# The first block's keys and queries with token groups outermost over the partitions

## The chip, the cores and the metric

The kernel runs on one core of a Trainium2 chip. A core has a matrix engine (PE, or TensorE), a vector engine (DVE), a scalar engine (ACT), GpSimd (POOL) and SyncE (SP), and moves data with 16 DMA engines. The metric is the device time of one execution in microseconds. Times of before and after are medians of several runs.

## The reference

Causal sliding-window attention with a linear distance bias, followed by a two-layer MLP with a squared ReLU. Cut to what matters:

```python
B, H, S, D = q.shape                       # 8, 8, 576, 64
scores = scale * q @ k.T                   # scale = 1 / sqrt(D)
bias = slopes[h] * -abs(i - j)
scores = where((i >= j) & (i - j < 128), scores + bias, -1e9)
attn = softmax(scores)
x = (attn @ v).transpose(0, 2, 1, 3).reshape(B * S, H * D)   # 4608 x 512
h = maximum(x @ w_in, 0.0)                 # w_in: 512 x 2048
out = (h * h) @ w_out                      # w_out: 2048 x 512
```

All inputs and the output are float32; the kernel computes in bfloat16 with float32 accumulation.

## The kernel before

The 576 tokens of each of the 8 batches are cut into four blocks of 128 and one of 64, which gives 40 blocks. Block numbers 0 to 7 are the first blocks of the eight batches (they attend only to themselves), the others follow by pairs of batches. For a block, q, k and v are loaded for all 8 heads with tokens on the partitions (tile `kq`, 128 x 1024, keys in the first half and queries in the second; `vf` or `vt` for the values). Keys and queries are transposed so that the head dimension lies on the partitions (`kqf` or `kqT`), the scores are formed (`s`, L499), exponentiated (L523), multiplied with a table of decays (`masks`), multiplied with the values (`pv`, L566), divided by their row sum into `x` and transposed again into `xT`. The MLP then works on groups of 512 tokens: an up-projection (`h`, L700 in units of 128 or 256 tokens for the first groups, L716 afterwards), ReLU and square into `g`, and a down-projection (`o`, L742).

The order of all instructions is written out when the program is built. Class `Plan` holds every task with its engine, an estimated duration, its dependencies and the ring buffers that it takes, and simulates the engines to choose an order; the tasks are then emitted in this order. The order, and the number of filler matmuls that `fill` puts on PE in planned gaps of the first 30 us (L252, on a zeroed tile `warm`), depend on the planner's estimates alone.

The list `FIRST` sets the order of the first loads: blocks 0 to 3 come ahead of the weights, then the quarters of w_in and w_out mixed with block 4, then blocks 5 to 7. Loads of GpSimd (queue q0) convert from float32 to bfloat16 on the way; at most eight of them are in flight, and a ninth waits for the first (`LANES`).

Block 0 differs. Its keys and queries are fetched as float32 into the tile `stage` by four loads (L373): keys and queries, each in two halves, one half on SP's queue and one on ACT's. VectorE then casts them into `kq` (L379), PE transposes them (L443), and `evac` (L451 to L458) copies the transposes into `kqf`. In `source` the 128 tokens are split into 32 groups g of four tokens i, and the eight heads into four pairs c of two heads r. A partition of `stage` holds one pair c and one group g: four tokens of 64 numbers, which is one run of 1 KB in memory for each head of the pair. Which partition it is follows from the order of c and g:

```python
        if split:
            return s.rearrange("(c r) (g i) d -> c g r (i d)", r=2, i=4)
```

So partition 32 c + g holds head pair c and token group g. After the transposes, the columns of the PSUM tile are in this order too, once for each i, and the evacuation sorts them into token order. The destination of a load is the 128 partitions of `stage`, 256 numbers in each.

Of the kernel before, what the change touches and what calls it, by code (L numbers as in the profile page):

```python
# [175 lines left out]
def kernel(  # L176
# [14 lines left out]
    C = d_model // 128  # L191
# [54 lines left out]
    def bank_of(slot, name):  # L246
        bank(slot, name)
        return slot

    def fill(task, slot):  # L250
        for _ in range(int(task.gap * FILL / 56.0) if task.gap > 200.0 else 0):
            nc.tensor.matmul(slot.tile[:, 0:128], warm[:, 0:128], warm[:, 0:128], start=True, stop=True)  # L252

    def tile_of(slot):
        return tiles[slot.tag][slot.idx]

    def act(n):
        return n * 0.95 + 115.0
# [4 lines left out]
    def dve_p(n, rate=1):  # L263
        return n / rate / 0.96 + 185.0

    def mm(n):
        return max(n, 66) / 2.4 + 2.5

    def copy(task, o, i):
        if task.eng == "DVE":  # L270
            nc.vector.tensor_copy(o, i)  # L271
        else:
            nc.scalar.activation(o, i, AF.Copy)  # L273
# [76 lines left out]
    def source(t, m, split=False):  # L350
        b, kb = seq[m]
        s = t[b, :, kb * 128:kb * 128 + blk[kb], :]
        if split:
            return s.rearrange("(c r) (g i) d -> c g r (i d)", r=2, i=4)
        return s.rearrange("h s d -> s h d")

    def load_block(m, key):
# [10 lines left out]
        if m == 0:  # L368
            t_l = []
            for i, src in enumerate((k, q)):  # L370
                for r, (eng, e) in enumerate((("SP", nc.sync), ("ACTQ", nc.scalar))):
                    def fetch(i=i, src=src, r=r, e=e):
                        e.dma_start(view(stage, i)[:, r], source(src, m, split)[:, :, r])  # L373
                    t_l.append(plan.add({eng: 450.0}, key + 0.1 * i, fetch, dma=330.0, lat=1000.0,
                                        name=f"l{'kq'[i]}{m}.{r}"))

            def cast_kq(i):
                w = slice(i * d_model, (i + 1) * d_model)
                nc.vector.tensor_copy(kq[s_kq[m].idx][:, w].rearrange("s (i r d) -> s r i d", i=4, d=D),  # L379
                                      stage[:, w].rearrange("s (r i d) -> s r i d", r=2, d=D))  # L380
            c_k = plan.add({"DVE": 480.0}, key, lambda: cast_kq(0), t_l[0:2], [s_kq[m]], name=f"ck{m}")
            c_q = plan.add({"DVE": 480.0}, key, lambda: cast_kq(1), t_l[2:4] + [c_k], name=f"cq{m}")
            t_kq[m] = [c_k, c_q]
        else:
            def fetch_kq():
                for i, src in enumerate((k, q)):
                    nc.gpsimd.dma_start(view(kq[s_kq[m].idx], i), source(src, m, split))  # L387
            t_kq[m] = [plan.add({"POOL": 1780.0}, key, fetch_kq, [], [s_kq[m]], dma=2 * ns,
                                name=f"lkq{m}", count=2)]

        def fetch_v():
            nc.gpsimd.dma_start(tile_of(s_v[m])[0:n, :, 0:D], source(v, m))  # L392
# [29 lines left out]
    def transpose_kq(m, due):  # L422
        n = blk[seq[m][1]]
        kb = seq[m][1]
        sT = s_kqT[m] = Slot("kqT" if kb else "kqT0")
        split = m == 0
        if m >= N_PE:
            def flip():
                nc.sync.dma_start_transpose(out=tile_of(sT)[:, :, 0:n], in_=kq[s_kq[m].idx][0:n, :])
            t_f = plan.add({"SP": 1500.0}, due - 60, flip, t_kq[m] + [t_zero if kb == HALF else None], [sT],  # L430
                           [s_kq[m]], dma=1700.0 * n / 128, name=f"kqT{m}")
            t_kqT[m] = [[t_f], [t_f]]
            return
        t_tp, evs = [None, None], [[], []]
        for i in range(2):
            st = Slot(TP if m else "o")

            def tp(i=i, st=st):
                fill(t_tp[i], bank_of(st, "tp"))
                st.tile = st.tile.bitcast(BF16)  # L440
                src = kq[s_kq[m].idx][:, i * d_model:(i + 1) * d_model]
                for j in range(C):
                    nc.tensor.transpose(st.tile[:, j * 128:(j + 1) * 128],  # L443
                                        src[:, j * 128:(j + 1) * 128], ident)
            t_tp[i] = plan.add({"PE": 4 * mm(128)}, due - 60 + i, tp,
                               [t_ident, t_tp[0] if i else last["tp"], t_kq[m][min(i, len(t_kq[m]) - 1)]],
                               [st] if i else [st, sT], [s_kq[m]] if i else [], name=f"tp{m}.{i}")

            pieces = [(0, C // 2), (C // 2, C)] if i and m == 0 else [(0, C)]
            for c0, c1 in pieces:  # L450
                def evac(i=i, st=st, c0=c0, c1=c1, e=len(evs[i])):  # L451
                    o = tile_of(sT)[:, i * C + c0:i * C + c1, 0:n]
                    if split:
                        src = st.tile[:, 0:512].rearrange("p (i c g) -> p c g i", i=4, c=C)[:, c0:c1]
                        o = o.rearrange("p c (g i) -> p c g i", i=4)
                    else:
                        src = st.tile[:, 0:512].rearrange("p (c s) -> p c s", c=C)[:, c0:c1, 0:n]
                    copy(evs[i][e], o, src)  # L458
                w = (c1 - c0) * n
                evs[i].append(plan.add({"ACT": act(w), "DVE": dve_p(w, 1 if split else 2)}, due - 58, evac,  # L460
                                       [t_tp[i]] + evs[i], [], [st], name=f"ev{m}.{i}"))
        last["tp"] = t_tp[1]
        t_kqT[m] = [[evs[0][0], evs[1][0]], evs[0] + evs[1]]
# [339 lines left out]
```

## Time and profile before

| | before |
|---|---|
| time, median of 3 runs | 321.18 us (320.49 to 322.58) |
| span of the profiled execution | 320.1 us |
| PE busy | 304.7 us (95%) |
| weight loads of PE (PEld) busy | 177.6 us (55%) |
| DVE busy | 175.3 us (55%) |
| ACT busy | 168.8 us (53%) |
| POOL busy | 105.4 us (33%) |
| moved by DMA | 39.54 MB |

A matmul's end is modelled, so the busy time of PE is an upper figure for useful work, and filler matmuls count as busy. In the parts of the profile shown below, a line of the chain of waits has start, length and what it was; a line of the timeline has start, length, engine, line of the kernel, operation, output and input, and in brackets the idle time before it and what ended it. A queue line has the number of packets, the megabytes and the time of its packets as a share of 16 engines' span.

### The profile page before, as it was taken

How to read it: one execution, taken by the hardware profiler on the slowest of the kernel's cores; microseconds unless marked ns; L12 is line 12 of the kernel's file. 1: busy time of each engine (PE TensorE's matmuls, PEld its weight loads, DVE VectorE, ACT ScalarE, POOL GpSimd, SP SyncE). 2: the span in 40 equal slices, each digit the busy share in tenths (PEclk: the TensorE clock that was granted, in tenths of full speed). 3: DMA queues.
4: the chain of work that ended last, by engine and by line, in shares of the span. 5: the costliest groups of instructions: out<-in, count | busy, mean ns of one | idle time of the engine just before them, and what ended most of it. 6: DMA issues, size and time to landing. Idle time of an engine off the chain costs nothing.

```text
span 320.1 us, 7110 instructions
## 1 busy us (share of the span) xinstructions
PE 304.7 (95%) x2776; PEld 177.6 (55%) x2820; DVE 175.3 (55%) x495; ACT 168.8 (53%) x324; POOL 105.4 (33%) x131
## 2 busy tenths in 40 slices
PE   4698999999999999999999999999999999999994
PEld 1596876777767645555545455554554444444442
DVE  2366446867767766677676667675764222222211
ACT  3356466666776327766666666645662444344300
POOL 8652579364352864411955105500000000000000
PEclk9999999999999999999999999999999999999998
DMA  9999999999999999997999929991121100010112
GB/s 105 122 200 202 189 160 188 145 158 166 159 157 166 187 176 163 156 164 141 151 187 170 161 67 156 161 163 52 38 60 37 66 33 33 37 33 33 66 68 66
DMA packets 165682, 39.54 MB, mean 124 GB/s; under 512 B 156304, under 2 KB 161168, under 8 KB 165648
## 3 DMA queue, kind: packets, MB, share of 16 engines
q0 software_dynamic: 114656, 18.10, 87.2%
q1 hardware_dynamic: 50728, 20.72, 34.7%
q8 instruction: 22, 0.36, 0.5%
q10 hardware_dynamic: 264, 0.26, 0.3%
q14 instruction: 12, 0.10, 0.1%
HBM read 36.70 MB, written 9.44 MB: 144 GB/s over the span
## 4 chain that ended last, share of the span: by engine, by line
PE 92%; DMA 3%; ACT 1%; issue 1%; DVE 1%; ACTq 0%
PE o L742 38%; PE h L716 25%; PE h L700 13%; PE pv L566 6%; PE s L499 5%; DMA stage<-in_q_dram 3%; PE tp L443 1%; PE tp L252 1%; ACT P L523 1%; PE xp L608 1%; ACT rt L671 1%; PE pv L252 0%; ACTq L373 0%; PE s L252 0%; PE xp L252 0%
## 5 line engine op out<-in xcount | busy, mean ns | idle before, releaser
L742 PE MATMUL o<-w_out_sb,g 128*128 128x512 bf16 (+2 forms) x568 | 138.8, 373 | 2.7 <-DVE g L662 1.1
L671 ACT ACTIVATE rt<-h 128x512 bf16<-128x512 f32 x144 | 86.2, 608 | 94.8 <-PE h L716 64.1
L662 DVE TENSOR_TENSOR g<-rt 128x512 bf16<-128x512 bf16 x144 | 60.0, 421 | 70.2 <-ACT rt L671 70.0
L716 PE MATMUL h<-xT,w_in_sb 128*128 128x512 bf16 x364 | 95.4, 379 | 0.9
L742 PEld LDWEIGHTS <-g 128*128 128x128 bf16 x592 | 54.2, 98 | 57.7 <-DVE g L662 1.4
L523 ACT ACTIVATE P<-s 128x512 bf16<-128x512 f32 (+1 forms) x132 | 66.5, 595 | 16.0 <-PE s L499 16.0
L716 PEld LDWEIGHTS <-w_in_sb 128*128 128x128 bf16 x384 | 35.0, 98 | 38.8
L531 DVE TENSOR_TENSOR P<-P,masks 128x512 bf16<-128x512 bf16 (+1 forms) x104 | 42.1, 413 | 15.4 <-ACT P L523 11.2
L700 PE MATMUL h<-xT,w_in_sb 128*128 128x128 bf16 (+1 forms) x512 | 46.4, 246 | 0.0
L392 POOL DMA_DIRECT2D vt<-in_v_dram x32 | 27.1, 850 | 54.0 <-PE pv L566 44.9
L387 POOL DMA_DIRECT2D kq<-in_k_dram x39 | 33.6, 860 | 28.8 <-DMA kqT<-kq 21.1
L700 PEld LDWEIGHTS <-w_in_sb 128*128 128x128 bf16 x512 | 38.3, 98 | 4.7 <-issue 0.4
L387 POOL DMA_DIRECT2D kq<-in_q_dram x39 | 33.7, 863 | 9.5 <-DMA w_out_sb<-in_moe_w_out_dram 3.6
L588 DVE TENSOR_TENSOR x<-pv,rec 128x256 bf16<-128x256 f32 (+1 forms) x80 | 33.7, 422 | 2.9 <-DVE rec L584 0.3
L566 PEld LDWEIGHTS <-P 128*128 128x128 bf16 (+1 forms) x576 | 26.0, 101 | 13.9 <-DVE x L588 1.7
L584 DVE RECIPROCAL rec<-pv 128x4 f32<-128x4 f32 (+1 forms) x80 | 14.2, 178 | 19.8 <-PE pv L566 17.6
L566 PE MATMUL pv<-vt,P 128*128 128x65 bf16 (+1 forms) x448 | 24.3, 194 | 0.2
L271 DVE COPY osb<-o 128x512 f32<-128x512 f32 (+2 forms) x17 | 11.2, 661 | 17.0 <-PE o L742 16.8
L273 ACT ACTIVATE osb<-o 128x512 f32<-128x512 f32 x20 | 11.9, 597 | 9.3 <-PE o L742 9.0
L499 PEld LDWEIGHTS <-kqT 64*128 64x128 bf16 x448 | 12.4, 94 | 7.4 <-issue 7.4
L499 PE MATMUL s<-kqT 64*128 64x128 bf16 (+1 forms) x256 | 15.6, 210 | 0.0
L443 PE MATMUL tp<-ident,kq 128*128 128x128 bf16 x64 | 6.2, 242 | 5.8 <-DVE kq L379 5.7
(41 smaller groups left out, 108.1 us busy)
## 6 DMA issues: line engine op xcount, KB each, us to landing
out_dram<-osb SPq DMA_DIRECT2D x32, 256.0 KB, 5.0
kq<-in_k_dram POOLq DMA_DIRECT2D x31, 128.0 KB, 7.5
kq<-in_q_dram POOLq DMA_DIRECT2D x31, 128.0 KB, 7.6
vt<-in_v_dram POOLq DMA_DIRECT2D x24, 128.0 KB, 7.1
w_in_sb<-in_moe_w_in_dram POOLq DMA_DIRECT2D x4, 512.0 KB, 13.4
w_out_sb<-in_moe_w_out_dram POOLq DMA_DIRECT2D x4, 512.0 KB, 14.2
vf<-in_v_dram POOLq DMA_DIRECT2D x8, 128.0 KB, 9.3
out_dram<-osb SPq DMA_DIRECT2D x6, 128.0 KB, 5.3
```

The costliest lines, as they stand in the source:

```text
L387: nc.gpsimd.dma_start(view(kq[s_kq[m].idx], i), source(src, m, split))
L392: nc.gpsimd.dma_start(tile_of(s_v[m])[0:n, :, 0:D], source(v, m))
L499: nc.tensor.matmul(sS[2 * g2 + r].tile[:, jj * 256 + c0:jj * 256 + c0 + w], tile_of(s_kqT[mk])[rows, c, :], tile_of(s_kqT[mq])[rows, C + c ...
L523: nc.scalar.activation(flat(Pt[sP.idx]), sS[i].tile.rearrange("p (j t) -> p j t", j=2)[:, :, lo:hi], AF.Exp, bias=0.0, scale=scale)
L531: nc.vector.tensor_tensor(flat(Pt[sP.idx]), flat(Pt[sP.idx]), flat(masks), op=ALU.mult)
L566: nc.tensor.matmul(sv.tile[0:n, hi * (D + 1):(hi + 1) * (D + 1)], Pt[sP.idx][:, place(h)].rearrange("p t q -> p (t q)")[:, w], tile_of(s_v ...
L588: nc.vector.tensor_tensor(xt[sx.idx][0:n, hf * 256:(hf + 1) * 256].rearrange("p (h e) -> p h e", h=4), heads(sv)[0:n, :, 0:D], sr.tile[0:n ...
L662: nc.vector.tensor_tensor(o, i, i, op=ALU.mult)
L671: nc.scalar.activation(srt.tile, slot.tile, AF.Relu, bias=0.0, scale=1.0)
L700: nc.tensor.matmul(slot.tile[:, f * w:(f + 1) * w], w_in_sb[:, cc, fc * 128:(fc + 1) * 128], xT[:, cc, lo:lo + w], start=cc == 0, stop=cc ...
L716: nc.tensor.matmul(slot.tile, w_in_sb[:, cc, fc * 128:(fc + 1) * 128], xT[:, cc, g * 512:(g + 1) * 512], start=cc == 0, stop=cc == C - 1)
L742: nc.tensor.matmul(slot.tile[:, 0:hi - lo], gt[:, fc, t * 128:(t + 1) * 128], w_out_sb[:, fc, lo:hi], start=fc == 0, stop=fc == FCB - 1)
```

## The change

In the source view of block 0 the order of c and g is exchanged, so that partition 4 g + c holds head pair c and token group g, and the slowest dimension of the loads' source has 32 entries instead of 4. This is meant to let these loads use all 16 DMA engines. The evacuation of the transposes reads its columns in the new order. Nothing else differs: the planner gets the same estimates and so writes the same order, and the load order with four blocks ahead of the weights stands already in the kernel before.

```diff
         if split:
-            return s.rearrange("(c r) (g i) d -> c g r (i d)", r=2, i=4)
+            return s.rearrange("(c r) (g i) d -> g c r (i d)", r=2, i=4)
         return s.rearrange("h s d -> s h d")
...
                     if split:
-                        src = st.tile[:, 0:512].rearrange("p (i c g) -> p c g i", i=4, c=C)[:, c0:c1]
+                        src = st.tile[:, 0:512].rearrange("p (i g c) -> p c g i", i=4, c=C)[:, c0:c1]
                         o = o.rearrange("p c (g i) -> p c g i", i=4)
```

## The prediction
> **What bounds the kernel now.** I read the page's chain first, then the same chain restricted to the first 45 us in order of time. The page:
>
> ```profile
> PE 92%; DMA 3%; ACT 1%; issue 1%; DVE 1%; ACTq 0%
> ```
>
> TensorE bounds the run, and the 3% of DMA is one single piece at the start. The chain in order of time (start us, us, what):
>
> ```profile
> 0.74 1.16 ACTq L373
> 1.90 0.03 issue
> 1.93 8.69 DMA stage<-in_q_dram
> 10.62 0.02 issue
> 10.64 0.44 DVE kq L379
> 11.09 0.05 issue
> 11.13 0.61 PE tp L443 x4
> ...
> 22.34 0.27 PE h L252 x3
> 22.62 1.79 PE h L700 x32
> ```
>
> Block 0's queries take until 10.62 to land; then cast, transpose, and from 11.13 on the chain stays on PE until the first up-projection. Is PE doing work there or waiting? The table by stretches (us, then busy us and instruction count of PE, PEld, DVE, ACT, POOL, the granted clock, DMA share, GB/s):
>
> ```profile
> 4.80:11.13 6.33, 0.61 (x4) 0.35 (x5) 1.41 (x3) 0.77 (x4) 3.76 (x6) 1.00 2.08 182
> 11.13:17.31 6.18, 6.18 (x64) 5.79 (x65) 3.06 (x10) 2.47 (x7) 5.87 (x8) 1.00 1.40 112
> 17.31:22.45 5.14, 5.14 (x99) 4.57 (x97) 3.77 (x17) 3.08 (x8) 2.93 (x4) 1.00 1.26 202
> 22.45:45.00 22.55, 21.26 (x316) 18.34 (x318) 12.94 (x45) 13.34 (x30) 10.41 (x13) 1.00 1.66 187
> 45.00:320.00 275.00, 267.93 (x2295) 147.48 (x2332) 153.09 (x416) 146.93 (x272) 78.44 (x95) 1.00 1.18 117
> ```
>
> PE is busy 0.61 of the 6.33 us before 11.13, and without a gap from 11.13 to 22.45 (76 of those matmuls are the fillers of L252, whose number is fixed when the program is built). Afterwards it is 94% and 97% busy. So a shift of the moment 11.13 is a shift of everything, unless a load that does not shift comes in the way.
>
> **Why the queries are late.** The queues of the first 12 us (packets, MB, share of 16 engines):
>
> ```profile
> q0 software_dynamic: 7066, 0.89, 116.5%
> q10 hardware_dynamic: 264, 0.26, 8.1%
> q1 hardware_dynamic: 264, 0.26, 7.1%
> ```
>
> Each hardware queue carries two of the four 128 KB loads of block 0. 256 packets are the 1 KB rows; the other 8 are 4-byte completion writes, four per load. So each load runs on four engines. In the trace's completion records the last k load lands at 6.87 and the last q load at 10.62. The same records show what this does to the GpSimd loads: of the 16 shares of block 0's v, twelve land from 4.92 to 5.73 and four from 10.47 to 10.80. Those four engines then work off their backlog: about 0.85 us per 128 KB load and 2.55 us per 512 KB load, so the last shares of w_in's first quarter land at 20.79, those of the first w_out quarter at 23.34. A load counts as landed with its last share. The GpSimd line of the timeline shows it too:
>
> ```profile
> 7.58 0.94 POOL L387 DMA_DIRECT2D kq<-in_k_dram  x1
> 11.08 0.88 POOL L387 DMA_DIRECT2D kq<-in_q_dram  x1 [2.57 <-DMA vf<-in_v_dram]
> ```
>
> The ninth load waits 2.57 us for v0, the first of the eight that are in flight.
>
> [...] the clock record starts at 17.31, 6.2 us after PE's unbroken work begins, and fillers go from 0.107 us each to about 0.06. [...] the first cast took 0.92 us while GpSimd issued loads, the second 0.43 while it waited.
>
> **The change, part by part.**
>
> Source view. With g (32) outermost, [...] same 512 rows of 1 KB, same four instructions, issued at the same times. Load time: a 1 KB packet takes 0.046 us on an engine (most of the packet records), so 512 packets are 23.6 us of engine time, 5.9 us on four engines and 1.5 us on sixteen. The first packet goes out at 2.20, and between 2.26 and 3.97 single packets take 0.4 to 1.38 us; I leave a stall of 0.5 to 1.4 us on every engine. The k loads then end near 2.2 + 0.75 + (0.5 to 1.4), plus about 0.3 us from last packet to completion: 3.75 to 4.65, I take 4.35. The q loads need another 0.75 us and meet GpSimd's packets, which begin at 3.59; between 6.3 and 10 the hardware packets went at 61 ns instead of 48 beside those. 4.6 to 6.5; I take 5.2.
>
> Casts on VectorE. Both now fall in a time when GpSimd issues without pause, so I charge 0.92 for each (0.43 is the other bound): k 4.35 to 5.27, q 5.27 to 6.2. Transpose of the queries starts at 6.3 instead of 11.13: **4.8 us earlier**; with 0.43 for the casts and an early q 5.5, with q at 6.5 3.6.
>
> Evacuation of the transposes (L454). Source step of g from 1 to 4 and of c from 32 to 1 elements; the innermost step stays 128, and so do instruction and element count. 0.69 on VectorE and 0.66 for the two on ACT stay; no row shows another stride, [...] I take 0.
>
> GpSimd loads. The four engines lose 5.8 us of block (start at 9.75, counted back from 20.79 by 10 x 0.85 + 2.55), and all sixteen get about 1 us of HW packets that still lie after 3.6. The twelve free engines landed the eighth load by 11.85; two more at 0.86, the weights at 2.55, and 0.5 to 1 us of sharing give 16.6 to 17.1 for w_in's first quarter: **4.2 us earlier** than 20.79 (3.7 to 4.7). The wait of 2.57 us disappears, as v0 lands by about 6.5 while the ninth load comes up at 8.5. Queued behind it are v3 and all weights, which move with it.
>
> Does the PE then meet the weights? In before it uses each well after landing: first quarter in 20.79, used 22.45 (1.65 spare); w_out's second quarter in 28.42, used 29.69 (1.3, the least); w_in's fourth in 38.82, used about 40.4 (1.6). So PE can move 4.2 + 1.3 = 5.5 us; 4.8 fits, with 0.7 left. Block 1's k and q (11.46 and 12.30) come at about 7 to 8.3, their transposes want them at 9.0; block 3's q comes near 13.4 and is wanted at 14.6. Those waits are covered.
>
> [...]
>
> Output stores, DMA transposes and all later loads are untouched and follow PE; the group loop from 45 us on has 97% PE and nothing new to wait for. Sum: 321.18 - 4.8 + 0.1 for small losses = 316.5.
>
> **The rivals.**
> 1. Forecast, 0.68: 316.5.
> 2. More, 0.12: fast casts, q near 4.6[...] move PE by more than the weights allow; the limit is 5.5 to 6: 315.4. For it: the second cast's 0.43. Against: GpSimd no longer pauses.
> 3. Part of it, 0.12: q lands near 7 because GpSimd's packets hold it up on every engine, or the weights move only 1.5 us and PE catches up with them: 1.5 + 1.3 = 2.8, so 318.4. For it: 61 ns against 48. Against: on the four shared engines the hardware packets kept most of the throughput.
> 4. Hidden anyway, 0.04: a wait that I don't see keeps the first up-projection at 22.45: 321.2. Against: PE has no gap from 11.13 on.
> 5. Slower, 0.04: [...] If every newly touched pair costs a stall like the four seen at the start (0.49, 1.38, 0.42 and 0.62, mean 0.73), that is 16 for the four loads: q lands at 2.2 + 1.5 + 16 x 0.73 + 0.3 = 15.7, 5.1 later than now, and the time is 326.3. Against: the other three loads touch new heads too, and after 4.3 no hardware packet takes more than 0.1 us.
>
> **How the numbers follow.** Cases 1 and 2 are faster by over 1% (3.2 us): 0.80. Cases 3 and 4 are within: 0.16. Case 5: 0.04. The range holds 1 with its ends (gains of 3.6 to 5.5), 2, and nearly all of 3: 314.9 to 318.6, which leaves out cases 4 and 5 and tails.
>
> **What would show it.** Right: 288 packets in each hardware queue (256 + 2 x 16), q landing near 5, the tp transposes of block 0 near 6.3, no wait of GpSimd for v0, the first up-projection near 17.6, PE busy as long as before in all. A first L700 near 17.6 with a gap in PE before it would say the weights bind (case 3). Wrong: stage still landing after 8, or PE gaps of more than 1 us between 18 and 45.

## The result and the profile after

| | before | after |
|---|---|---|
| time, median | 320.94 us (320.49 to 322.58, 4 runs) | 318.03 us (317.12 to 318.91, 4 runs) |
| ratio to before, 95% interval | | 0.9900 (0.9853 to 0.9947) |
| the same, measured again later | 321.29 us (11 runs) | 318.29 us (6 runs), ratio 0.9898 (0.9873 to 0.9923) |
| span of the profiled execution | 320.1 us | 316.7 us |

The change makes the kernel 2.9 us faster. The forecast was 4.7 us (316.5 us, range 314.9 to 318.6). The intervals of the two measurements leave 1.7 to 4.7 us and 2.5 to 4.1 us for the gain.

The loads do what they were meant to do. The queues of the first 12 us of the kernel after, columns as before:

```profile
q0 software_dynamic: 9001, 1.14, 148.5%
q1 hardware_dynamic: 288, 0.26, 7.9%
q10 hardware_dynamic: 288, 0.26, 7.9%
```

288 packets are 256 rows and 32 completions, sixteen for each load. And GpSimd's queue has moved 9001 packets instead of 7066 in the same 12 us. The last share of the keys lands at 3.55 us (6.87 before), that of the queries at 6.24 (10.62). All sixteen shares of block 0's v land from 4.71 to 6.71, where four of them had waited until 10.80. GpSimd's line of the timeline no longer has the wait for the ninth load:

```profile
8.43 0.95 POOL L387 DMA_DIRECT2D kq<-in_q_dram  x1
9.30 0.95 POOL L392 DMA_DIRECT2D vf<-in_v_dram  x1
10.16 0.84 POOL L340 DMA_DIRECT2D w_in_sb<-in_moe_w_in_dram  x1
```

The chain of the page shows what became of it:

```profile
PE 80%; DMA 14%; POOL 4%; issue 0%; DVE 0%; POOLq 0%; SPq 0%
```

Before, PE held 92% of the chain and DMA 3%, one load of block 0. Now DMA has 14%. That the number is larger doesn't mean more DMA time; it means that PE now waits for DMA somewhere late enough for the chain to run back through it. Restricted to 40 to 62 us and put in order of time, the chain says where:

```profile
40.47 0.85 POOL kq L387
41.32 7.53 DMA kq<-in_q_dram
...
48.93 9.20 DMA kqT<-kq
58.13 0.04 issue
58.17 0.62 PE s L499 x16
```

The scores of block 8, the first block that is transposed by DMA and not by PE, wait for that transpose. In the kernel before this wait did not exist. PE's own lines in the timeline show it, after two smaller waits for weights that are new as well:

```profile
17.28 1.96 PE L700 MATMUL h<-xT,w_in_sb 128*128 128x128 bf16 x32 [0.82 <-DMA w_in_sb<-in_moe_w_in_dram]
...
24.95 1.02 PE L742 MATMUL o<-w_out_sb,g 128*128 128x512 bf16 x4 [0.26 <-DMA w_out_sb<-in_moe_w_out_dram]
...
58.17 0.23 PE L499 MATMUL s<-kqT,kqf 64*128 64x128 bf16 x2 [1.36 <-DMA kqT<-kq]
```

PE has the same 2820 weight loads in the same order in both kernels, so the start of each can be compared between two traces, and the difference is how far PE is ahead at that moment. After against the first profile of before:

| place | before, us | after, us | ahead by, us |
|---|---|---|---|
| transpose of block 0's queries (L443) | 11.13 | 7.06 | 4.07 |
| transpose of an x tile, the second of them (L608) | 21.50 | 15.34 | 6.16 |
| first up-projection (L700) | 22.40 | 17.28 | 5.12 |
| second quarter of w_out (L742) | 29.69 | 24.95 | 4.74 |
| an up-projection before block 8's scores (L700) | 55.57 | 50.82 | 4.75 |
| block 8's scores (L499) | 61.49 | 58.17 | 3.32 |
| near the end (L742) | 313.79 | 310.33 | 3.46 |

So PE was ahead by some 4.75 us, close to the 4.8 of the forecast, from 25 us to 58 us, and lost 1.4 at one wait. But the table ends at 3.46 and the medians differ by 2.9, so this comparison isn't yet the whole account. The experiments are about both points.

### The profile page after: what moved, and what is told of

It is laid out like the page before. It is cut to its first block, busy times and chain, and to the rows that moved or that the text cites. A ratio compares the mean times of both kernels' runs of the same rounds, so it can differ in the third digit from the quotient of the medians.

```text
span 316.7 us, 7154 instructions
## 1 busy us (share of the span) xinstructions
PE 305.4 (96%) x2820; PEld 175.3 (55%) x2820; DVE 175.2 (55%) x495; ACT 169.0 (53%) x324; POOL 105.4 (33%) x131
## 4 chain that ended last, share of the span: by engine, by line
PE 80%; DMA 14%; POOL 4%; issue 0%; DVE 0%; POOLq 0%; SPq 0%
PE o L742 35%; PE h L716 27%; PE h L700 8%; PE pv L566 5%; DMA w_in_sb<-in_moe_w_in_dram 5%; PE s L499 5%; DMA vf<-in_v_dram 3%; DMA kqT<-kq 3%; DMA kq<-in_q_dram 2%; POOL kq L387 2%; POOL vf L392 1%; POOL w_out_sb L343 1%; POOL w_in_sb L340 0%; POOL dist L287 0%; DVE osb L271 0%
## 5 line engine op out<-in xcount | busy, mean ns | idle before, releaser
L742 PE MATMUL o<-w_out_sb,g 128*128 128x512 bf16 (+2 forms) x592 | 142.9, 374 | 1.3 <-DVE g L662 1.1
L716 PE MATMUL h<-xT,w_in_sb 128*128 128x512 bf16 x384 | 96.9, 380 | 0.0
L742 PEld LDWEIGHTS <-g 128*128 128x128 bf16 x592 | 54.2, 98 | 58.1 <-DVE g L662 1.4
L523 ACT ACTIVATE P<-s 128x512 bf16<-128x512 f32 (+1 forms) x132 | 66.5, 595 | 17.1 <-PE s L499 17.0
L700 PE MATMUL h<-xT,w_in_sb 128*128 128x128 bf16 (+1 forms) x512 | 46.4, 246 | 0.8 <-DMA w_in_sb<-in_moe_w_in_dram 0.8
L700 PEld LDWEIGHTS <-w_in_sb 128*128 128x128 bf16 x512 | 38.3, 98 | 5.5 <-DMA w_in_sb<-in_moe_w_in_dram 1.0
L499 PEld LDWEIGHTS <-kqT 64*128 64x128 bf16 x448 | 12.5, 94 | 7.4 <-issue 7.0
L499 PE MATMUL s<-kqT 64*128 64x128 bf16 (+1 forms) x256 | 15.6, 210 | 0.0
L499 PE MATMUL s<-kqT,kqT 64*128 64x128 bf16 (+1 forms) x192 | 11.4, 210 | 0.0
```

Source lines behind the costliest of these rows:

```text
L499: nc.tensor.matmul(sS[2 * g2 + r].tile[:, jj * 256 + c0:jj * 256 + c0 + w], tile_of(s_kqT[mk])[rows, c, :], tile_of(s_kqT[mq])[rows, C + c ...
L523: nc.scalar.activation(flat(Pt[sP.idx]), sS[i].tile.rearrange("p (j t) -> p j t", j=2)[:, :, lo:hi], AF.Exp, bias=0.0, scale=scale)
L700: nc.tensor.matmul(slot.tile[:, f * w:(f + 1) * w], w_in_sb[:, cc, fc * 128:(fc + 1) * 128], xT[:, cc, lo:lo + w], start=cc == 0, stop=cc ...
L716: nc.tensor.matmul(slot.tile, w_in_sb[:, cc, fc * 128:(fc + 1) * 128], xT[:, cc, g * 512:(g + 1) * 512], start=cc == 0, stop=cc == C - 1)
L742: nc.tensor.matmul(slot.tile[:, 0:hi - lo], gt[:, fc, t * 128:(t + 1) * 128], w_out_sb[:, fc, lo:hi], start=fc == 0, stop=fc == FCB - 1)
```

## The experiments

Theory A was: the gain is given back at block 8's scores. Rival B: the stream of loads came only 3.5 us earlier and holds PE to that, so that another wait for a load or a DMA transpose takes the place of this one within some 10 us. The first four kernels belong together.

**Taking away the wait at block 8.** The scores of block 8 read another block's transposes, which are there already.

```diff
+                                ka, qa = (0 if x == 8 and ms[0] == 8 else x for x in (mk, mq))
                                 nc.tensor.matmul(sS[2 * g2 + r].tile[:, jj * 256 + c0:jj * 256 + c0 + w],
-                                                 tile_of(s_kqT[mk])[rows, c, :], tile_of(s_kqT[mq])[rows, C + c, 0:w],
+                                                 tile_of(s_kqT[ka])[rows, c, :], tile_of(s_kqT[qa])[rows, C + c, 0:w],
```

> The changed kernel, except that the scores of block 8 (its own and those against its predecessor) read the transposes of block 0 in place of block 8's own; block 8's output and what follows from it is therefore other. Same instructions in the same order, but the first score matmuls no longer wait for the DMA transpose of block 8. Theory A (the gain of 4.75 us that PE has at 57 us is given back at that one wait): PE stays about 4.7 us ahead of the kernel before past 58 us, and the time is 316.4 to 316.9, 1.1 to 1.5 less than the changed kernel. Rival B (the whole stream of loads came only 3.5 us earlier and holds PE to that anywhere): another wait for a load or a DMA transpose takes its place within some 10 us, PE is 3.4 to 3.6 ahead afterwards, and the time is 317.7 to 318.3.

Measured: 318.10 us, ratio 0.9899 (0.9870 to 0.9928), as the changed kernel, and in B's range. But in its trace PE is 4.70 us ahead of the first profile of before at 58 us and still at 86, as A says; then it loses 0.53 at an up-projection at 91 us and 0.4 at a score matmul at 116 us. PE's waits from 60 to 125 us in this kernel (total, times, longest, in us):

```profile
PE h L701 <- DMA xT<-x: 0.5, 1, 0.5
PE o L743 <- issue: 0.3, 2, 0.2
```

The new wait is for a DMA transpose again, this time of x. The loss at 116 us is too short for this list; the chain leads from it over VectorE's writing of `x` to a DMA transpose of `x` that landed at 114.56. So A in its narrow form falls: with this wait gone, others of the same kind take its place. B named such waits too, but within 10 us, and these came 33 and 58 us later.

**Bringing the transpose forward.** The values of blocks 5 to 7, which aren't needed before about 46 us, are loaded after block 8's keys and queries. The emission is rearranged once the planner is done, so PE, VectorE and ACT keep their order.

```diff
     done = plan.order()
+    late = [t for t in done if t.name in ("lv5", "lv6", "lv7")]
+    done = [t for t in done if t not in late]
+    z = [t.name for t in done].index("lkq8") + 1
+    done[z:z] = late
```

> The changed kernel with the GpSimd loads of the values of blocks 5, 6 and 7 issued after the keys and queries of block 8 instead of before; everything else in the same order. Block 8's queries should land about 3 x 0.86 = 2.6 us earlier, near 46.2. Theory A1 (the transpose follows the landing of the queries): kqT of block 8 lands near 55.5, before PE wants it at 56.8, the wait of 1.36 us is gone, time 316.4 to 316.9. Theory A2 (the transpose's packets can't start before the backlog of GpSimd's loads has drained, at about 53 us in the changed kernel, and that moment stays): the transpose is issued 2.6 us earlier and still lands at 57 to 58, time 317.5 to 318.3.

Measured: 317.34 us, ratio 0.9880 (0.9853 to 0.9907), which lies between the two ranges, so the trace has to decide. The SP queue of this kernel in the timeline issues the transpose of block 8 at 44.30 instead of 48.93:

```profile
44.30 1.35 SPq L429 DMA_TRANSPOSE kqT<-kq  x1
```

It lands at 52.48, 8.2 us after its issue; in the kernel before that took 8.2 and in the kernel after 9.2. The transpose follows the landing of the queries, which come at 44.21 (A1); a fixed moment at which GpSimd's backlog is drained (A2) is not what it waits for. And PE's waits from 10 to 125 us have no transpose among them, neither block 8's nor a later one:

```profile
PE o L742 <- DVE g L662: 1.1, 1, 1.1
PE h L700 <- DMA w_in_sb<-in_moe_w_in_dram: 0.9, 1, 0.9
PE o L742 <- issue: 0.5, 3, 0.2
```

**The same in the kernel before,** as a control.

> The kernel before with the same later loads of the values of blocks 5 to 7. Theory A: in before the transpose of block 8 landed 1.8 us ahead of its use, so earlier loads are worth nothing: 320.6 to 321.3, no change. Rival B (the stream of loads held PE in before as well): 0.5 to 2 us faster, 319.0 to 320.4.

Measured: 321.23 us, ratio 1.0004 (0.9991 to 1.0016). Without the change, earlier transposes are worth nothing. The wait for block 8's is one that the change brought within reach.

**Half of the change.** Only the keys in the new order.

```diff
-            return s.rearrange("(c r) (g i) d -> g c r (i d)", r=2, i=4)
+            return s.rearrange("(c r) (g i) d -> g c r (i d)" if t is k else "(c r) (g i) d -> c g r (i d)", r=2, i=4)
...
-                        src = st.tile[:, 0:512].rearrange("p (i g c) -> p c g i", i=4, c=C)[:, c0:c1]
+                        src = st.tile[:, 0:512].rearrange("p (i c g) -> p c g i" if i else "p (i g c) -> p c g i", i=4, c=C)[:, c0:c1]
```

> Only the keys of block 0 in the new order, the queries in the old one, so the query loads run on four engines again. If the time on shared engines counts packet by packet: 64 packets on each of four engines at 0.046 to 0.061 us from about 3.1 us on, so the queries land at 6.5 to 7.5, transposed from about 7.9 (11.13 before, 7.06 after), and those four engines start GpSimd's loads near 6.7 (9.75 before): w_in's first quarter lands at 17.8 to 18.5 and the time is 318.0 to 319.2. Rival (what counts is only that no load is confined to four engines; two confined loads cost as much as four): the queries land after 9.5 and the time is 320.3 to 321.2.

Measured: 319.36 us, ratio 0.9942 (0.9919 to 0.9964), just above the range of the first theory, and far from the rival's. Each hardware queue has 276 packets (256 + 16 + 4). The queries land at 8.47, later than the 7.5 allowed for, and w_in's first quarter at 18.73. The dose counts: with two confined loads the ratio lies at 0.9942, with none at 0.9900, so two cost a little under half of what four do. In this trace no load holds PE up: its first up-projection starts at 19.86, 1.1 us after the quarter landed. What binds there is the later queries and PE's own work, with a full clock from 14.29 us on.

These four leave a gap: even without any wait for a transpose the gain is 3.6 us, not 4.7. One suspect is the yardstick, since the first profile of before, at 321.89 us, was 0.9 slower than the median. Two kernels were run again for a second profile.

> The kernel before once more, for a second execution with a profile. Its first profile had the full clock only from 17.31 us, and its time of 321.89 is 0.9 above the median of 320.97. Theory C [...]: with the full clock earlier, the first up-projection starts earlier than 22.45, but not before w_in's first quarter lands at about 20.8, and the span is 319.0 to 319.5. Rival: the clock comes at another time and the span stays within 0.3 of what the start of the up-projection gives otherwise, that is, the 0.9 us lie elsewhere in the run.

Measured: 321.17 us, span 319.4. In this execution PE had the full clock from 14.89 us, not from 17.31. The first up-projection starts 1.28 us earlier than in the first profile, at

```profile
21.17 1.95 PE L700 MATMUL h<-xT,w_in_sb 128*128 128x128 bf16 x32
```

with w_in's first quarter landed at 20.65. And PE's waits from 10 to 125 us have one that the first profile of this same program did not have:

```profile
PE o L742 <- DMA w_out_sb<-in_moe_w_out_dram: 0.5, 1, 0.5
```

Half of the 1.28 us is lost there; 0.58 is left at 29 us and 0.73 at the end. So the span is as theory C says, and the trace says more than expected: the loads can bind PE in the kernel before as well. The kernel before with the later values has the same wait in its trace, 0.6 us long. The 1.3 us that PE seemed to have in hand at the second quarter of w_out belonged to that one execution: just ahead of that place PE is 1.28 us earlier in the second profile, which uses them up, and the quarter landed 0.65 us later (29.07 against 28.42), which makes the wait.

How much of the 0.9 us the clock explains is less sure. The record has the mean granted clock of 54 more executions of the kernel before. In 33 of them it is below 0.99, as in the second profile (0.988); their median is 321.11 us. In the other 21 it is 0.995 or more, as in the first profile (0.996); their median is 321.27. Over many executions the difference is thus about 0.2 us, and in one of the three sessions it goes the other way.

> The changed kernel once more, for a second execution with a profile. Theory: the first up-projection again waits for w_in's first quarter (start 17.2 to 17.6 unless the clock comes after about 11 us), and what is given back is given back at waits for DMA transposes (kqT at 58 us, or xT at about 88 and 112 us), of a size that varies from run to run by up to 1.5 us; span 315.3 to 317.1. Rival: the wait of 1.36 us at block 8's scores is the same in each execution.

Measured: 317.57 us, span 315.8. Its first up-projection waits 0.97 us, for a w_in quarter that landed at 18.19 (17.23 in the first profile of after), so it starts at 18.23 and not at 17.2 to 17.6; block 8's transpose lands at 56.17, before it is wanted, and nothing is lost at 58 us or at any later transpose. So the theory had the span and the varying size right, but not the start, and the rival falls. The trace of the first profile of after shows the difference: fifteen of the sixteen shares of that transpose had landed by 56.74 and one at 58.13. So the size of what is given back varies, and in that execution it hung on a single late share. Against the second profile of before, PE is ahead by (the rows "timed again" are the profiles of two of the last three kernels below):

| | first up-projection | second w_out quarter | block 8's scores and to the end |
|---|---|---|---|
| after, first profile | 3.84 | 4.16 | 2.73 |
| after, second profile | 2.89 | 3.59 | 3.59 |
| after, timed again | 2.95 | 3.63 | 3.64 |
| values later, first profile | 3.64 | 4.38 | 4.38 |
| values later, timed again | 3.42 | 4.15 | 4.15 |

So in two of the three traces of the changed kernel no transpose holds PE up. These three executions took 318.46, 317.57 and 317.52 us; what the slower executions lose beyond that, up to 319.04, has no trace.

**Is it the clock that the change bought?** The kernel before with PE kept busy until the queries land:

```diff
-        for _ in range(N_WARM):
+        for _ in range(30):
```

> The kernel before with 30 warm-up matmuls instead of 8 at the start of PE, emitted without telling the planner, so that PE is busy until 9 to 11 us, where it otherwise waits for the queries, [...]. Theory (weights cap the gain): PE reaches the first up-projection at 20.8 to 21.2, waits there for w_in's first quarter (20.8), and the time is 320.4 to 321.0, at most 0.6 below the kernel before. Rival (the clock, not the loads, is what the change really bought): 318 to 319.5.

Measured: 322.21 us (21 runs), ratio 1.0016 (0.9999 to 1.0032), which is neither's range: no gain, perhaps a loss. The full clock comes at 4.76, and PE's waits from 10 to 125 us show how the earlier start is used up:

```profile
PE o L742 <- DVE g L662: 1.7, 2, 1.1
PE tp L443 <- DVE kq L379: 1.1, 1, 1.1
PE h L700 <- DMA w_in_sb<-in_moe_w_in_dram: 0.5, 1, 0.5
PE o L742 <- issue: 0.5, 3, 0.2
PE s L499 <- DMA kqT<-kq: 0.4, 1, 0.4
PE h L700 <- DMA xT<-x: 0.2, 1, 0.2
```

It is the pattern of the changed kernel, without the earlier loads: PE comes sooner and meets weights and transposes that do not. Ahead of the second profile of before by 1.26 us at the second x transpose, it is 0.48 behind from 95 us on. Why it ends behind was not settled. But an early clock alone brings no gain, so it is not what the change bought.

**Is it the stream of loads that binds at the start?** On top of the later values, one load is left out.

```diff
+    done = [t for t in done if t.name != "lv3"]
...
-                                         tile_of(s_v[mk])[:, h, 0:D + 1], start=mk == parts[0][1], stop=mk == m)
+                                         tile_of(s_v[2 if mk == 3 else mk])[:, h, 0:D + 1],
+                                         start=mk == parts[0][1], stop=mk == m)
```

> The kernel with the values of blocks 5 to 7 loaded later, and block 3's values not loaded at all (its attention reads block 2's values instead, so block 3's output is other). It takes 0.85 us of work out of the stream of loads ahead of the weights and changes nothing else. Theory D (in the first 30 us the stream of loads bounds the changed kernel, PE waits for each weight quarter): all weights land 0.85 us earlier, PE follows, 316.3 to 316.9, against 317.34 with only the later loads. Rival (PE and VectorE's own chain bounds it, the waits for weights are by-products): 317.2 to 317.6.

Measured: 316.93 us, ratio 0.9868 (0.9856 to 0.9881). In time this is in theory D's range, but the step is not clear of noise: the ratio is 0.0012 below that of the kernel with the later values, some 0.4 us, and the two intervals overlap. PE's waits from 10 to 125 us now have no DMA in them at all:

```profile
PE o L743 <- DVE g L663: 1.1, 1, 1.1
PE o L743 <- issue: 0.5, 3, 0.2
```

w_in's first quarter landed at 15.81 and PE used it at 17.03, so PE's own chain took over as the bound there (the full clock came at 11.13 in this execution). That the loads bind the changed kernel at its start is shown by the traces rather than by this time: in all three profiles of it, and in both with the values later, the first up-projection has waited 0.8 to 1.0 us and starts about 0.05 us after that quarter has landed, at 17.28 to 18.23. By these waits PE's own chain stands about a microsecond behind the loads as a bound.

**A version to keep.** The last three were timed side by side.

> The changed kernel, timed beside the next two: 317.6 to 318.4, as in its first measurement.

Measured: 318.29 us, ratio 0.9898 (0.9873 to 0.9923).

> The changed kernel with the values of blocks 5 to 7 loaded after the keys and queries of block 8, timed again beside the changed kernel: 317.1 to 317.6. Theory: 0.5 to 0.9 below the changed kernel, since the wait for block 8's DMA transpose and those after it are gone. Rival: the earlier difference was between two measurements, and it is within 0.2 here.

Measured: 317.79 us, ratio 0.9877 (0.9848 to 0.9907). The difference of 0.5 us agrees with the 0.69 of the first time, though the intervals overlap; over all executions on record the medians are 318.27 (11, the changed kernel) and 317.55 (9, the values later). That the transposes make this difference is not shown. Neither trace of the kernel with the values later waits for one, but neither does the trace of the changed kernel that was taken beside it; between those two traces PE's lead differs by 0.47 us at the first up-projection already, where their loads are still in the same order.

The third also moves block 4's values behind block 8's queries, and block 3's behind the second quarter of w_in:

```diff
+    late = [t for t in done if t.name in ("lv4", "lv5", "lv6", "lv7")]
+    v3 = [t for t in done if t.name == "lv3"]
+    done = [t for t in done if t not in late + v3]
     ...
+    z = [t.name for t in done].index("w_in1") + 1
+    done[z:z] = v3
```

> As the last, with block 4's values moved behind block 8's queries too, and block 3's values behind the second quarter of w_in. Computes the same as the reference, no load is left out. The first three weight quarters should land 0.85 us earlier; the second quarter of w_out, which the 24.95 us wait of the changed kernel is for, has the same work ahead of it as before. Theory (that quarter is what binds): 317.0 to 317.5, as the kernel with only the values of blocks 5 to 7 moved. Rival (the first quarter binds, as its 0.8 us wait suggests): 316.4 to 316.8.

Measured: 317.62 us, ratio 0.9878 (0.9851 to 0.9905), as the one before it. PE no longer waits for the first quarter of w_in but for the second of w_out:

```profile
PE o L742 <- DVE g L662: 1.1, 1, 1.1
PE o L742 <- DMA w_out_sb<-in_moe_w_out_dram: 0.9, 1, 0.9
```

The 0.9 us went from one wait to the other. Here the second quarter of w_out binds, which has as much work ahead of it as before, and a shuffle of what lies before it doesn't help.

## Why the prediction was right in its mechanism and too large in its size

- **What bounds the kernel: too simple.** "A shift of the moment 11.13 is a shift of everything, unless a load that does not shift comes in the way": the queries' transpose moved by 4.07 us, and the loads came in the way. The prediction named the sign of this: a first L700 near 17.6 with a gap in PE before it. It came at 17.28, after a gap of 0.82 us.
- **Four engines, then sixteen: right.** That the new order gives sixteen was the author's estimate; 288 packets in each queue show it, sixteen completions for each load. The stall at the first packets was overcharged: up to 3.3 us none took more than 0.26 us, and the keys landed at 3.55 instead of the 4.35 taken. The queries were undercharged: 6.24 instead of 5.2, near the upper end of the bounds. Beside GpSimd's first packets, from 3.3 to 5 us, four single packets took 0.37 to 0.78 us, more than 61 against 48 ns suggested. That it is the number of engines that counts is read from these records; the new order of rows on four engines was not run.
- **Casts: 0.73 and 0.67 us,** between the two bounds of 0.43 and 0.92. A fixed price was the wrong picture: in the traces a cast beside an issuing GpSimd ended 0.27 to 0.32 us after GpSimd went on to its next issue (the last section has the lines). For this reason the queries' transpose starts at 7.05 to 7.07 in six of the eight traces with keys and queries in the new order, though the queries landed at 6.00 to 6.45; 6.3 was taken.
- **Evacuation at nothing: right.** 0.67 us on VectorE (0.69 before), 0.66 for the two on ACT.
- **GpSimd loads: 3.6 us earlier in the first profile** (17.23 against 20.79), 2.5 between the second profiles (18.19 against 20.65); 4.2 was taken. This is the first term that was too large. Its own working, 16.6 to 17.1, gives 3.7 to 4.2 us, so 4.2 was the far end of it. And that working fits fifteen of the sixteen shares, which were in by 16.85 and 16.91; the last one came 0.4 and 1.3 us after them, and PE waits for the last.
- **"So PE can move 4.2 + 1.3 = 5.5 us; 4.8 fits": the step that failed.** The spare of 1.3 us was read off one execution, in which PE's clock came late. In the second profile of before, PE waits 0.5 us for that very quarter of w_out. Without spare, PE can move only as far as the loads: 3.6 to 4.2 us at that place instead of 4.8.
- **The moment of the full clock: no term in the sum, and the base was mixed.** In the kernel before, what an early clock gave was lost at later waits, in whole or in part: with PE kept busy it came at 4.76 us and brought no gain (ratio 1.0016), and where it came at 14.89 us instead of 17.31, of 1.28 us at the first up-projection 0.73 were left at the end. The moments of the forecast were taken from a profile of 321.89 us, and its gain was then taken off a median of 321.18.
- **"Output stores, DMA transposes and all later loads are untouched and follow PE": the second step that failed.** They are untouched, and they did not follow PE. Block 8's queries landed 2.6 us earlier (48.85 against 51.46) and the transpose, 9.2 us long instead of 8.2, 1.6 us earlier, where PE came 4.75 us earlier. That cost 1.4 us in one traced execution of the changed kernel and nothing in the two others. The 0.1 us "for small losses" stood for it.
- The sum from the runs: against the second profile of before, PE is 4.2, 3.6 and 3.6 us ahead at the weights in the three traces of the changed kernel; less 1.4, 0 and 0 at the transposes this is 2.7, 3.6 and 3.6. The medians say 2.9 and 3.0. The gain is thus that of the rival "Part of it", 2.8 us, and not one of the forecast's 3.6 to 5.5. That rival had the right kind of limit, the weights, though not its size: they came 2.5 to 3.6 us earlier and not 1.5, and the spare of 1.3 that it added was not there, so its number is in part luck.

Left open: why the DMA transposes take 8 to 9 us at this place. While loads run (60 to 130 us) the median from issue to landing of `kqT` is 7.5 us and of `xT` 7.3 in the kernel after; from 150 to 300 us it is 5.7 and 3.0. That goes with the traffic, 167 GB/s in the first stretch and 89 in the second, but no run took the traffic away. For single late shares the traces have a candidate, in the last section, which no run tested.

## What to carry to other kernels

Here four loads on four engines did not only land late themselves, at 10.62 us: block 0's v, queued by GpSimd, had twelve of its sixteen shares in by 5.73 and the other four at 10.47 to 10.80. So look at the last shares of the other loads and not only at the transfer that is to be made faster. One late share was enough for this: w_in's first quarter had fifteen in by 16.91 and the last at 18.19, and PE started on it at 18.23. When PE is to be moved forward, list what it will meet at each later wait. A transfer that waits for another transfer did not follow PE here: block 8's transpose came 1.6 us earlier where PE came 4.75 us earlier. And a spare time read from one profile belongs to that execution, on both sides, the engine's and the load's: before it is spent, check in a second profile that it is still there.

## What was not expected of the hardware

Beside the confined hardware loads in the kernel before, four shares of GpSimd's first load came late. These shares of block 0's v landed from 10.47 to 10.80, around the landing of the last hardware load at 10.62, while the twelve others were done by 5.73, 2.1 us after GpSimd's first packet (3.59). That the four are those on the confined engines is read from these times and not shown. The count agrees that GpSimd got little there: from 6.5 to 9.5 us its queue moved about 465 packets in each half microsecond, where in the kernel after it moves about 600 (588 to 616 from 5.5 us on), and twelve sixteenths of 600 are 450. In the kernel after, with the loads on sixteen engines, both gave way: 345 of the 512 rows went in the 1.3 us up to 3.5, just after GpSimd's packets begin, and the other 167 take until about 5.9; GpSimd moves 141 and 135 packets in the first two half microseconds.

The sixteenth share has a likely cause that the argument above doesn't use. In the second profile of after, at 16.15 us, one packet of 16 KB on a queue that the profile calls "instruction" took 0.95 us. Its line among the queues of the stretch from 16 to 17 us, columns as before:

```profile
q8 instruction: 1, 0.02, 5.9%
```

Fifteen shares of w_in's first quarter were in by 16.91, the last at 18.19, and each of the next three quarters also had one share 0.9 to 1.0 us behind the others. In the kernel without block 3's values that quarter was complete at 15.81, the packet came at 15.97, and the first late share is that of the next quarter (18.45, then 19.36). In the two profiles of before, the packet comes at 20.98 and 20.46; the next such packet came at 29.57 in the first, after the second quarter of w_out was in (28.42), and at 28.14 in the second, where fifteen shares were in by 28.45 and the last at 29.07. The record doesn't say on which engine a packet ran, so that this packet delays the share is read from the times and not shown.

The casts show how VectorE was held up beside GpSimd's issues. VectorE's and GpSimd's lines of the kernel after:

```profile
3.65 0.73 DVE L379 CAST kq<-stage 128x512 bf16<-128x512 f32 x1 [1.74 <-DMA stage<-in_k_dram]
4.10 0.90 POOL L392 DMA_DIRECT2D vf<-in_v_dram  x1
...
6.33 0.67 DVE L379 CAST kq<-stage 128x512 bf16<-128x512 f32 x1 [1.95 <-DMA stage<-in_q_dram]
6.70 0.93 POOL L392 DMA_DIRECT2D vf<-in_v_dram  x1
```

The casts end at 4.38 and 7.00, 0.28 and 0.30 us after GpSimd's next issue starts. Without block 3's values the second cast began at 6.10 and took 0.91 us, to 7.01. In the thirteen traces nineteen casts begin well within one issue of GpSimd and are still unfinished when the next starts, and all nineteen end 0.27 to 0.32 us after that start, whenever they began. In the two above the issue in which the cast began had ended by then, at 4.13 and 6.75. The two casts that met an issue in its first moments (at 5.82 and 5.92, issues from 5.83, both with the values later) took no more than 0.43 us, as the second cast of the kernel before did while GpSimd waited, so the first moments of an issue did not lengthen them. Why a cast is held up by an issue is not shown.

The clock record has both directions within the first 15 us. In the second profile of before the full clock was granted from 4.65 to 8.07 (3.41 us), taken back for 6.83 us and granted again at 14.89. The second stretch is twice the first, to 0.01 us, in this one execution.
